# Weights loaded by thirds, k and v in two passes, one ring of PSUM double banks, more dummy matmuls and a new order of steps in an attention and maxout kernel

## The chip, the cores and the metric

One core of one Trainium2 chip. The metric is the device time of one execution in microseconds (us), median of several. A profile gives the span of one execution; the time is the span plus about 1.8 us (175.5 and 177.35 for the same execution of the kernel before). Seven of the timed runs named below count as slow, over 1.5% above the fastest of their kernel: one of e5's 20, four of e9's 20, and one of four in each of e6 and e6b. The first figure given for these kernels is the median of all runs, and that of the fast ones stands beside it; the ratios use fast runs alone. One single run that has no state is said to be so.

## The reference

```python
# q, k, v: [8 batches, 8 heads, 576, 64]; phi: [8, 8, 576, 32]; all float32
a   = softmax(phi, over the 576 positions)
k_m = a^T k;  v_m = a^T v                    # 32 memory slots for each head
attn = softmax(q k_m^T / 8) v_m
x   = attn with the heads side by side       # [4608, 512]
h   = max(x w1, x w2, x w3)                  # 768 wide
out = h w_out                                # [4608, 512]
```

## The kernel before

The kernel never forms x. It folds v_m into the weights, batch by batch, so that the softmax weights are multiplied straight with (w1 - w3), (w2 - w3) and w3 w_out. A hand-made order of steps is issued; each letter is a step, `@` gives the batch. PE does the matmuls, ACT and DVE work element by element, and POOL issues loads. A matmul writes into PSUM; to evacuate a tile is to copy it out of PSUM with ACT or DVE. The buffers of a PSUM pool are used in turn, as a ring: a new tile takes the slot of the oldest one and waits until that is evacuated. A fold is the product of v_m with one block of weight columns. What this text needs of the steps: L0, L1, L2 load phi, k with v, and q; E is exp of phi; B the k and v products; Q transposes q on DVE; S scores; M, R, X the softmax (R is ln and exp on ACT); D0 to D3 the four folds; F0 to F11 the first FFN product and its max; T0 to T4 output tiles; W and O build w3 w_out; V subtracts w3; Z is dummy matmuls that keep the clock up.

```python
acc_pool = tile_pool(name="accp", bufs=3, space=PSUM)   # double banks
one_pool = tile_pool(name="onep", bufs=2, space=PSUM)   # single banks
w_sb = const.tile([P, NP, 3, DF], BF16, name="w_sb")
# ... cut ...
load_ph(0); load_kv(0); load_q(0)       # all but phi(0) are issued by POOL, in this order
load_w(2); load w_out                   # w3, then w_out
load_w(0); load_w(1)                    # w1, w2
load_ph(1); load_kv(1); load_q(1)
# ... cut ...
EVAC = {"D": "asaa", "T": "vaava"}      # who takes folds 0..3 and output tiles 0..4 out of PSUM

def evacuate(kind, n, out_, in_):
    e = EVAC[kind][n]
    if e == "s":                                             # split: one bank each
        nc.scalar.copy(out=out_[:, 0], in_=in_[:, 0])        # ACT
        nc.vector.tensor_copy(out=out_[:, 1], in_=in_[:, 1]) # DVE
    elif e == "a": nc.scalar.copy(out=out_, in_=in_)
    else:          nc.vector.tensor_copy(out=out_, in_=in_)
# ... cut ...
for w in """
    E@0 L0@2 Z26@0 B@0 N@0 Z5@0 K@0 Q0@0 Q1@0 L2@2 L1@2 Z18@0 W1@0 W0@0 S@0 M0@0 R0@0
    W2@0 M1@0 O1@0 O0@0 V0@0 R1@0 O3@0 X0@0 X1@0 D0@0 V2@0 O2@0 F6@0 ...
""".split(): ...
for b in range(2, B - 1):
    run(b, "F6 F0 T4- F7 F4 F1 F2 F10 F3 F8 F5 F9 T2- S+ Q0++ B++ L1++++ D3+ E+++")
    run(b, "L0+++++ N++ T3- M0+ R0+ M1+ F11 X0+ T0 R1+ X1+ Q1++ L2++++ D0+ D2+ D1+")
    run(b, "T1 K++")
```

The softmax here doesn't subtract the row's maximum and nothing guards it: scores larger than these inputs give would overflow.

## Time and profile before

| | kernel before |
|---|---|
| time, median | 176.04 us (175.83 to 176.35, 3 runs) |
| profiled execution | span 175.5 us, 177.35 us with its start and end: above every timed run in this row |
| a later profile of the same kernel | span 174.0 us, 175.8 us |

The prediction shows the lines that its argument rests on. Two things that it does not show turned out to matter. The first is in the timeline of POOL, the engine that issues nearly all loads (columns: start us, length us, engine, line, what it issues, and in brackets how long POOL stood still before it and for whom):

```profile
70.66 0.76 POOL L92 DMA_DIRECT2D ph<-in_phi_dram  x1
...
80.85 0.76 POOL L92 DMA_DIRECT2D ph<-in_phi_dram  x1 [1.69 <-ACT ln L327]
...
101.52 0.74 POOL L107 DMA_DIRECT2D qq<-in_q_dram  x1 [6.08 <-DVE qT L271]
```

The last phi is issued at 80.85, and the last load of all, q, at 101.52, after it. POOL stands still for several us before a load whose buffer is not free yet; whatever is behind it in POOL's order stands still too. The second is in the list of what PE waits for, before (total us, times, longest):

```profile
PE acc L383 <- ACT wp L156: 0.9, 2, 0.7
PE acc L383 <- DVE wp L154: 0.9, 2, 0.6
```

These are the only waits for evacuated folds in the whole kernel.

### The profile page before, as it was taken

The page shows a single profiled execution, that of the slowest core. Times are in us where ns is not written, and L with a number is a line of the kernel's source. Part 1 is how long each engine was busy: PE and PEld are TensorE (multiplying, and loading weights), DVE is VectorE, ACT ScalarE, POOL GpSimd, SP SyncE. Part 2 cuts the span into 40 slices and gives each one's busy share as a digit, 9 for nine tenths or more (in the row PEclk, how much of TensorE's full clock was granted, in tenths as well). Part 3 has the DMA queues.
Part 4 walks back from the last instruction along what each step waited for, and adds up shares of the span by engine and source line. Part 5 has one row for each costly group of instructions (what it writes and reads, how often), then busy time and mean ns, then how long its engine had stood idle before and what let it go on. Part 6 is the DMA issues. An engine that isn't in the chain of part 4 may idle for free.

```text
span 175.5 us, 4464 instructions
## 1 busy us (share of the span) xinstructions
PE 162.1 (92%) x1921; PEld 89.1 (51%) x1921; DVE 103.9 (59%) x160; ACT 108.0 (62%) x162; POOL 28.3 (16%) x43
## 2 busy tenths in 40 slices
PE   7959599797999998999999999999999999999990
PEld 2334353363466544754665456547564565466430
DVE  6408216698489567767775837587748362556110
ACT  4100248945976889569949965798479648952210
POOL 7951111113303230222103010000000000000000
PEclk9999969999999999999999999999999999999999
DMA  5999999999999999999999999312013201311333
GB/s 151 169 205 209 208 211 273 212 253 232 216 320 246 238 257 246 287 236 234 321 239 277 246 250 245 100 73 108 4 63 119 86 35 63 121 60 63 119 119 121
DMA packets 21973, 31.76 MB, mean 181 GB/s; under 512 B 1216, under 2 KB 16576, under 8 KB 21952
## 3 DMA queue, kind: packets, MB, share of 16 engines
q0 software_dynamic: 16080, 21.43, 63.4%
q1 hardware_dynamic: 5728, 9.90, 16.0%
q8 instruction: 15, 0.25, 0.5%
q10 hardware_dynamic: 144, 0.13, 0.2%
q14 instruction: 6, 0.05, 0.1%
HBM read 39.32 MB, written 9.44 MB: 278 GB/s over the span
## 4 chain that ended last, share of the span: by engine, by line
PE 73%; ACT 9%; DMA 8%; DVE 4%; POOL 2%; issue 1%; DVEq 0%; POOLq 0%
PE acc L383 25%; PE po L411 24%; DMA w_sb<-in_moe_w_dram 8%; PE po L420 7%; PE wps L358 4%; PE kvp L219 3%; PE sm L314 2%; ACT wp L156 2%; PE po L175 2%; POOL kvo L99 1%; PE sc L293 1%; ACT h L393 1%; DVE hT L395 1%; PE po L429 1%; ACT r L333 1%
## 5 line engine op out<-in xcount | busy, mean ns | idle before, releaser
L383 PE MATMUL acc<-attn,wp 128*128 128x288 bf16 x384 | 52.6, 286 | 2.1 <-ACT wp L156 0.9
L411 PE MATMUL po<-wo_sb,hT 128*128 128x512 bf16 x216 | 52.6, 380 | 0.0
L395 DVE TENSOR_TENSOR hT<-acc,h 128x576 bf16<-128x576 f32 x48 | 35.1, 754 | 18.0 <-PE acc L383 12.2
L383 PEld LDWEIGHTS <-wp 128*128 128x128 bf16 x384 | 36.5, 97 | 16.2 <-issue 2.5
L393 ACT ACTIVATE h<-acc 128x576 bf16<-128x576 f32 x48 | 29.4, 652 | 12.8 <-PE acc L383 11.9
L411 PEld LDWEIGHTS <-hT 128*128 128x128 bf16 x216 | 20.0, 98 | 24.2 <-issue 4.3
L156 ACT CAST wp<-wps 128x1024 bf16<-128x1024 f32 x24 | 23.7, 1016 | 3.2 <-PE wps L358 3.2
L156 ACT COPY ot<-po 128x512 f32<-128x512 f32 x19 | 11.3, 596 | 21.2 <-PE po L420 15.7
L158 DVE COPY ot<-po 128x512 f32<-128x512 f32 x16 | 11.1, 692 | 20.2 <-PE po L420 20.2
L271 DVE STREAM_TRANSPOSE qT<-qq 128x1152 bf16<-128x1152 bf16 x16 | 21.6, 1363 | 0.6 <-DMA qq<-in_q_dram 0.6
L302 ACT ACTIVATE e<-sc 128x576 bf16<-128x576 f32 x16 | 9.6, 660 | 15.4 <-PE sc L293 15.4
L420 PE MATMUL po<-wp,attn 128*128 128x512 bf16 x64 | 19.0, 379 | 0.0
L143 PE MATMUL po<-warm 128*128 128x512 bf16 x49 | 12.7, 419 | 1.2 <-DVE warm L131 1.2
L338 DVE TENSOR_TENSOR attn<-e,r 128x576 bf16<-128x576 bf16 x16 | 12.0, 751 | 2.0 <-ACT r L333 1.9
L99 POOL DMA_DIRECT2D kvo<-in_k_dram x9 | 6.7, 747 | 31.4 <-PE kvp L219 23.4
L208 ACT ACTIVATE e<-ph 128x1152 bf16<-128x1152 f32 (+1 forms) x9 | 9.7, 1072 | 2.7 <-DMA ph<-in_phi_dram 2.7
L333 ACT ACTIVATE r<-ln 128x576 f32<-128x576 f32 x16 | 10.9, 684 | 0.5
L327 ACT ACTIVATE ln<-sm 128x576 f32<-128x576 f32 x16 | 10.3, 646 | 1.4 <-PE sm L314 1.4
L219 PE MATMUL kvp<-kvo,e 64*32 64x192 bf16 x576 | 8.4, 243 | 2.3 <-DMA kvo<-in_v_dram 2.3
L420 PEld LDWEIGHTS <-attn 128*128 128x128 bf16 x64 | 6.3, 98 | 7.0
L107 POOL DMA_DIRECT2D qq<-in_q_dram x8 | 6.0, 749 | 22.4 <-DVE qT L271 12.6
L219 PEld LDWEIGHTS <-e 64*32 64x32 bf16 x576 | 7.1, 90 | 4.1 <-issue 4.0
(43 smaller groups left out, 107.2 us busy)
## 6 DMA issues: line engine op xcount, KB each, us to landing
out_dram<-ot SPq DMA_DIRECT2D x35, 256.0 KB, 2.2
qq<-in_q_dram POOLq DMA_DIRECT2D x8, 576.0 KB, 18.1
ph<-in_phi_dram POOLq DMA_DIRECT2D x7, 576.0 KB, 17.5
kvo<-in_k_dram POOLq DMA_DIRECT2D x7, 576.0 KB, 16.2
kvo<-in_v_dram POOLq DMA_DIRECT2D x7, 576.0 KB, 19.0
w_sb<-in_moe_w_dram POOLq DMA_DIRECT2D x3, 768.0 KB, 19.7
wo_sb<-in_moe_w_out_dram POOLq DMA_DIRECT2D x1, 768.0 KB, 17.4
ph<-in_phi_dram SPq DMA_DIRECT2D x2, 288.0 KB, 3.5
```

Source lines behind the costliest of these rows:

```text
L143: nc.tensor.matmul(po[:, 0:BANK], lhsT=warm[:, 0:P], rhs=warm, start=True, stop=True)
L156: nc.scalar.copy(out=out_, in_=in_)
L158: nc.vector.tensor_copy(out=out_, in_=in_)
L219: nc.tensor.matmul(kvp[M * j : M * (j + 1), a, 0 : 3 * D], lhsT=s["e"][r, j, c, :], rhs=kv[r, :, j, c, :], start=(c == 0), stop=(c == NC - 1),
L271: nc.vector.transpose(out=s["qT"][:, j].rearrange("p j c h r -> p (j c h r)"), in_=loaded[b]["q"][:, j].rearrange("p j c d -> p (j c d)"),)
L333: nc.scalar.activation(out=r, in_=ln, func=AF.Exp, scale=-1.0)
L338: nc.vector.tensor_tensor(out=attns[b // 2][:, g, (b % 2) * S : (b % 2 + 1) * S], in0=s["e2"][:, g, 0:S], in1=s["r", g], op=ALU.mult,)
L383: nc.tensor.matmul(acc[:, h, 0:SH], lhsT=wps[b][:, g, w * DF + ft * P : w * DF + (ft + 1) * P], rhs=attn[:, g, c0 : c0 + SH], start=(g == ...
L393: nc.scalar.activation(out=h1, in_=a, func=AF.Relu)
L395: nc.vector.tensor_tensor(out=hT[:, ft, (b % 2) * S : (b % 2 + 1) * S].rearrange("p (h n) -> p h n", h=2), in0=a, in1=s["h1", ft], op=ALU.max,
L411: nc.tensor.matmul(po, lhsT=hT[:, fc, c0 : c0 + P], rhs=wo_sb[:, fc, :], start=(fc == 0), stop=False,)
L420: nc.tensor.matmul(po, lhsT=attn[:, g, c0 : c0 + P], rhs=wp3s[b][:, g, :], start=False, stop=(g == NG - 1),)
```

## The change

The intent: let weights become usable earlier, in thirds of columns that belong together; start on k while v is still under way; give output tiles and FFN tiles one common ring of PSUM; fill the early gaps of PE so that the clock stays up. With this came another division of the evacuations between ACT and DVE, and a new order of all steps. The diff is abridged.

```diff
-    tile_pool(name="accp", bufs=3, PSUM); tile_pool(name="onep", bufs=2, PSUM)
+    tile_pool(name="accp", bufs=4, PSUM)                # one ring of four double banks
-    w_sb = const.tile([P, NP, 3, DF], BF16)
+    w12 = const.tile([P, NP, NT, 2, DF // NT], BF16)    # NT = 3; w1 and w2 side by side per third
+    w3 = const.tile([P, NP, DF], BF16)
     load_ph(0)
-    load_kv(0) in halves; load_q(0); load_w(2); load w_out; load_w(0); load_w(1)
-    load_ph(1); load_kv(1); load_q(1)
+    load_q(0); load_one(k, 0); load_one(v, 0)
+    for n in 0, 1, 2: load_w(2, n); load_w(0, n); load_w(1, n)
+    load_wo(all); load_ph(1); load_q(1); load_one(k, 1); load_one(v, 1)
-    EVAC = {"D": "asaa", "T": "vaava"}
+    EVAC = {"D": "ssaa", "T": "aavaa"}
     # w_diff: one subtraction per third, w3 broadcast over w1 and w2
     # att_kv, norm, transpose: k and v separately (G, H, J) in batches 0 and 1
-    E@0 L0@2 Z26@0 B@0 N@0 Z5@0 K@0 ... Z18@0 W1@0 ...                  (49 dummies)
+    E@0 Z38@0 G0@0 Q1@0 Z9@0 G1@0 H0@0 H1@0 Q0@0 J0@0 L2@2 Z8@0 ...     (73 dummies)
+    ... M0@4 L2@7 R0@4 T1@3 X1@4 L0@7 E@6 T0@3 X0@4 K@5 L1@7            (explicit up to batch 4)
-    for b in range(2, B - 1): run(b, "F6 F0 T4- ...")
+    for b in range(4, B - 1): run(b, "F8 L2++++ F9 F6 F10 F2 F7 T4- S+ F0 F11 E+++ ...")
```

More of the change, by code (lines that the diff above doesn't have):

```diff
@@ L43 @@
     BANK = 512
+    NT = 3
+    CT = DF // NT
     const = ctx.enter_context(tc.tile_pool(name="const", bufs=1))
@@ L50 @@
     acc_pool = ctx.enter_context(
-        tc.tile_pool(name="accp", bufs=3, space=bass.MemoryType.PSUM)
-    )
-    one_pool = ctx.enter_context(
-        tc.tile_pool(name="onep", bufs=2, space=bass.MemoryType.PSUM)
+        tc.tile_pool(name="accp", bufs=4, space=bass.MemoryType.PSUM)
     )
@@ L68 @@
         kvos.append(kvo)
-    w_sb = const.tile([P, NP, 3, DF], BF16, name="w_sb")
+    w12 = const.tile([P, NP, NT, 2, DF // NT], BF16, name="w12")
+    w3 = const.tile([P, NP, DF], BF16, name="w3")
     w3T = const.tile([P, FT, NP, P], BF16, name="w3T")
@@ L92, in load_ph, with load_one, load_kv @@
             nc.gpsimd.dma_start(out=dst, in_=by_pair(phi, b))
-    def load_kv(b):
+    def load_one(src, b):
         kv = kvos[b % 2]
         loaded.setdefault(b, {})["kv"] = kv
-        for h in halves if b == 0 else [slice(0, NP)]:
-            for i, src in enumerate((k, v)):
-                nc.gpsimd.dma_start(
-                    out=kv[:, i].rearrange("p j c d -> p j (c d)")[:, h],
-                    in_=by_pair(src, b)[:, h],
-                )
+        nc.gpsimd.dma_start(
+            out=kv[:, 1 if src is k else 0].rearrange("p j c d -> p j (c d)"),
+            in_=by_pair(src, b),
+        )
+    def load_kv(b):
+        load_one(k, b)
+        load_one(v, b)
     def load_q(b):
@@ L109, in load_q, with load_w, load_wo @@
         )
-    def load_w(i):
+    def load_w(i, n):
         w = (moe_w1, moe_w2, moe_w3)[i]
+        c = slice(n * CT, (n + 1) * CT)
         nc.gpsimd.dma_start(
-            out=w_sb[:, :, i], in_=w.rearrange("(j p) f -> p j f", p=P)
+            out=w3[:, :, c] if i == 2 else w12[:, :, n, i],
+            in_=w.rearrange("(j p) f -> p j f", p=P)[:, :, c],
+        )
+    def load_wo(fs):
+        nc.gpsimd.dma_start(
+            out=wo_sb[:, fs], in_=moe_w_out.rearrange("(t p) c -> p t c", p=P)[:, fs]
         )
     load_ph(0)
-    load_kv(0)
     load_q(0)
-    load_w(2)
-    nc.gpsimd.dma_start(out=wo_sb, in_=moe_w_out.rearrange("(t p) c -> p t c", p=P))
+    load_one(k, 0)
+    load_one(v, 0)
+    load_w(2, 0)
     ident = const.tile([P, P], BF16, name="ident")
     make_identity(nc, ident)
-    load_w(0)
-    load_w(1)
+    load_w(0, 0)
+    load_w(1, 0)
+    load_w(2, 1)
+    load_w(0, 1)
+    load_w(1, 1)
+    load_w(2, 2)
+    load_w(0, 2)
+    load_w(1, 2)
+    load_wo(slice(0, FT))
     load_ph(1)
-    load_kv(1)
     load_q(1)
+    load_one(k, 1)
+    load_one(v, 1)
     warm = const.tile([P, BANK], BF16, name="warm")
@@ L139, in warm_up @@
     def warm_up(n):
-        po = one_pool.tile([P, DM], FP32, name="po", tag="one")
+        po = acc_pool.tile([P, DM], FP32, name="po", tag="acc")
         for _ in range(n):
@@ L161, in w3_t @@
     def w3_t(f2):
-        pt = one_pool.tile([P, 2, NP, P], BF16, name="pt", tag="one")
+        pt = acc_pool.tile([P, 2, NP, P], BF16, name="pt", tag="acc")
         for i in range(2):
@@ L167, in w3_t @@
                 nc.tensor.transpose(
-                    pt[:, i, j, :], w_sb[:, j, 2, f * P : (f + 1) * P], ident
+                    pt[:, i, j, :], w3[:, j, f * P : (f + 1) * P], ident
                 )
@@ L172, in w3_o @@
     def w3_o(j):
-        po = one_pool.tile([P, DM], FP32, name="po", tag="one")
+        po = acc_pool.tile([P, DM], FP32, name="po", tag="acc")
         for f in range(FT):
@@ L182, in w3_o @@
         nc.scalar.copy(out=w3o[:, j, :], in_=po)
-    w12 = w_sb[:, :, 0:2].rearrange("p j i f -> p j (i f)")
     def w_diff(n):
-        c = n * BANK
-        while c < (n + 1) * BANK:
-            e = min((n + 1) * BANK, (c // DF + 1) * DF)
-            nc.vector.tensor_tensor(
-                out=w12[:, :, c:e],
-                in0=w12[:, :, c:e],
-                in1=w_sb[:, :, 2, c % DF : c % DF + e - c],
-                op=ALU.subtract,
-            )
-            c = e
+        nc.vector.tensor_tensor(
+            out=w12[:, :, n],
+            in0=w12[:, :, n],
+            in1=w3[:, :, n * CT : (n + 1) * CT].unsqueeze(2).to_broadcast([P, NP, 2, CT]),
+            op=ALU.subtract,
+        )
     st = {}
@@ L208, in att_exp, with att_kv @@
         nc.scalar.activation(out=s["e"][:, js], in_=loaded[b]["ph"][:, js], func=AF.Exp)
-    def att_kv(b, js=range(NP)):
+    def att_kv(b, js=range(NP), slabs=slice(0, 3)):
         s = st[b]
@@ L219, in att_kv @@
                     nc.tensor.matmul(
-                        kvp[M * j : M * (j + 1), a, 0 : 3 * D],
+                        kvp[M * j : M * (j + 1), a, D * slabs.start : D * slabs.stop],
                         lhsT=s["e"][r, j, c, :],
-                        rhs=kv[r, :, j, c, :],
+                        rhs=kv[r, slabs, j, c, :],
                         start=(c == 0),
@@ L226, in att_kv, with att_k_norm @@
                     )
-    def att_kv_norm(b):
+    def att_k_norm(b):
         s = st[b]
         kvp = s["kvp"]
-        rden = work.tile([P, NG], FP32, name="rden")
+        rden = s["rden"] = work.tile([P, NG], FP32, name="rden")
         nc.vector.reciprocal(out=rden, in_=kvp[:, :, 2 * D])
-        kvn = work.tile([P, 3, P], BF16, name="kvn")
-        nc.vector.tensor_tensor(
-            out=kvn[:, 0].rearrange("p (a d) -> p a d", a=NG),
-            in0=kvp[:, :, D : 2 * D],
-            in1=rden.unsqueeze(2).to_broadcast([P, NG, D]),
-            op=ALU.mult,
-        )
+        kn = s["kn"] = work.tile([P, 2, P], BF16, name="kn")
         for g in range(NG):
-            kn = kvn[:, 1:3, HP * g : HP * (g + 1)]
             nc.vector.tensor_scalar_mul(
-                out=kn.rearrange("p h (t d) -> p h t d", t=2),
-                in0=kvp[:, g, 0:D]
+                out=kn[:, :, HP * g : HP * (g + 1)].rearrange("p h (t d) -> p h t d", t=2),
+                in0=kvp[:, g, D : 2 * D]
                 .rearrange("p (h d) -> p h d", h=2)
@@ L250, in att_kv_norm, with att_v_norm, att_kv_t @@
             )
-        s["kvn"] = kvn
-    def att_kv_t(b):
+    def att_v_norm(b):
         s = st[b]
-        ps = one_pool.tile([P, 3, P], BF16, name="kvtp", tag="one")
-        for n in range(3):
-            nc.tensor.transpose(ps[:, n], s["kvn"][:, n], ident)
-        kvt = work.tile([P, 3, P], BF16, name="kvt")
-        nc.vector.tensor_copy(out=kvt, in_=ps)
-        s["kvt"] = kvt
+        vn = s["vn"] = work.tile([P, NG, D], BF16, name="vn")
+        nc.vector.tensor_tensor(
+            out=vn,
+            in0=s["kvp"][:, :, 0:D],
+            in1=s["rden"].unsqueeze(2).to_broadcast([P, NG, D]),
+            op=ALU.mult,
+        )
+    def att_kv_t(b, k_=True, v_=True):
+        s = st[b]
+        ps = acc_pool.tile([P, 3, P], BF16, name="kvtp", tag="acc")
+        n = slice(0 if k_ else 2, 3 if v_ else 2)
+        if k_:
+            for h in range(2):
+                nc.tensor.transpose(ps[:, h], s["kn"][:, h], ident)
+        if v_:
+            nc.tensor.transpose(ps[:, 2], s["vn"].rearrange("p a d -> p (a d)"), ident)
+        if "kvt" not in s:
+            s["kvt"] = work.tile([P, 3, P], BF16, name="kvt")
+        nc.vector.tensor_copy(out=s["kvt"][:, n], in_=ps[:, n])
     def att_q(b, n):
@@ L294, in att_score @@
                             sc[a][M * j : M * (j + 1), t, 0:SH],
-                            lhsT=kvt[r, 1 + h, M * j : M * (j + 1)],
+                            lhsT=kvt[r, h, M * j : M * (j + 1)],
                             rhs=qT[r, j, :, h, :],
@@ L359, in fold @@
                     ps[M * j : M * (j + 1), a, :],
-                    lhsT=s["kvt"][r, 0, M * j : M * (j + 1)],
-                    rhs=w12[r, j, n * BANK : (n + 1) * BANK] if n < 3 else w3o[r, j, :],
+                    lhsT=s["kvt"][r, 2, M * j : M * (j + 1)],
+                    rhs=w12[r, j, n].rearrange("p i c -> p (i c)") if n < 3 else w3o[r, j, :],
                     start=True,
@@ L375, in ffn1 @@
         ft, w = n // 2, n % 2
+        k0 = (ft * P // CT * 2 + w) * CT + ft * P % CT
         if b // 2 not in hts:
@@ L384, in ffn1 @@
                     acc[:, h, 0:SH],
-                    lhsT=wps[b][:, g, w * DF + ft * P : w * DF + (ft + 1) * P],
+                    lhsT=wps[b][:, g, k0 : k0 + P],
                     rhs=attn[:, g, c0 : c0 + SH],
@@ L407, in ffn2 @@
         hT, attn = hts[b // 2], attns[b // 2]
-        po = one_pool.tile([P, DM], FP32, name="po", tag="one")
+        po = acc_pool.tile([P, DM], FP32, name="po", tag="acc")
         c0 = S - HP if t == 4 else (b % 2) * (S + HP) + t * P
@@ L458, in issue @@
             "E": lambda: [att_exp(b, h) for h in (halves if b == 0 else [slice(0, NP)])],
-            "B": lambda: [att_kv(b, range(NP)[h]) for h in (halves if b == 0 else [slice(0, NP)])],
-            "N": lambda: att_kv_norm(b),
+            "B": lambda: att_kv(b),
+            "N": lambda: (att_k_norm(b), att_v_norm(b)),
+            "G": lambda: att_kv(b, slabs=(slice(1, 3), slice(0, 1))[i]),
+            "H": lambda: (att_k_norm, att_v_norm)[i](b),
+            "J": lambda: att_kv_t(b, k_=i == 0, v_=i == 1),
             "K": lambda: att_kv_t(b),
@@ L481 @@
     for w in """
-        E@0 L0@2 Z26@0 B@0 N@0 Z5@0 K@0 Q0@0 Q1@0 L2@2 L1@2 Z18@0 W1@0 W0@0 S@0 M0@0 R0@0
-        W2@0 M1@0 O1@0 O0@0 V0@0 R1@0 O3@0 X0@0 X1@0 D0@0 V2@0 O2@0 F6@0 F2@0 F4@0 V1@0 F0@0
-        D2@0 D1@0 F7@0 F3@0 E@1 L0@3 F8@0 F1@0 F9@0 F5@0 F10@0 F11@0 B@1 L1@3 D3@0 N@1 K@1
-        D0@1 Q1@1 Q0@1 L2@3 D2@1 D1@1 T2@0 S@1 T0@0 E@2 L0@4 M0@1 R0@1 M1@1 X0@1 R1@1 X1@1
-        T3@0 T1@0 Q1@2 F0@1 F8@1 F1@1 F9@1 F6@1 F2@1 D3@1 B@2 L1@4 Q0@2 L2@4 F4@1 N@2 F7@1
-        K@2 F10@1 F3@1 S@2 F5@1 F11@1 M1@2 E@3 L0@5 M0@2 R1@2 R0@2 T0@1 D0@2 X0@2 D2@2 B@3
-        L1@5 N@3 X1@2 T1@1 D1@2 D3@2 Q0@3 Q1@3 L2@5 K@3 E@4 L0@6
+        E@0 Z38@0 G0@0 Q1@0 Z9@0 G1@0 H0@0 H1@0 Q0@0 J0@0 L2@2 Z8@0 S@0 W0@0 M1@0 V0@0 Z3@0
+        W1@0 M0@0 R1@0 J1@0 R0@0 X1@0 V1@0 X0@0 L0@2 Z12@0 D1@0 D0@0 Z3@0 F6@0 W2@0 F0@0
+        V2@0 F4@0 F7@0 F1@0 D2@0 F2@0 F3@0 Q1@1 F8@0 F10@0 O2@0 E@1 O0@0 F5@0 O1@0 L1@2 O3@0
+        F9@0 F11@0 Q0@1 D3@0 G0@1 H0@1 T3@0 J0@1 L0@3 G1@1 H1@1 J1@1 L2@3 S@1 D2@1 L1@3 T0@0
+        M1@1 Q0@2 M0@1 R1@1 T2@0 R0@1 D3@1 X1@1 X0@1 D0@1 D1@1 T1@0 F8@1 F0@1 Q1@2 F4@1 E@2
+        F9@1 F6@1 F1@1 F5@1 B@2 F2@1 L0@4 N@2 F7@1 F10@1 K@2 E@3 F3@1 L1@4 F11@1 Q1@3 S@2
+        T3@1 M0@2 R0@2 Q0@3 M1@2 T1@1 R1@2 X1@2 X0@2 T4@1 T2@1 D0@2 D2@2 B@3 N@3 D1@2 F2@2
+        F8@2 F3@2 K@3 E@4 F4@2 F9@2 F6@2 F5@2 S@3 F10@2 F7@2 L2@5 F0@2 F11@2 M0@3 F1@2 R0@3
+        M1@3 R1@3 L0@5 T0@1 D1@3 D0@3 X0@3 X1@3 D3@2 B@4 L2@4 D2@3 T1@2 L0@6 F2@3 N@4 F10@3
+        F4@3 F3@3 K@4 F0@3 F11@3 F6@3 D1@4 D3@3 Q1@4 D3@4 E@5 Q0@4 L1@5 L1@6 F8@3 T3@2 F9@3
+        T0@2 S@4 D0@4 B@5 N@5 D2@4 F5@3 L2@6 F7@3 F1@3 Q1@5 Q0@5 M1@4 T2@2 R1@4 M0@4 L2@7
+        R0@4 T1@3 X1@4 L0@7 E@6 T0@3 X0@4 K@5 L1@7
     """.split():
@@ L491 @@
         issue(int(b), n)
-    for b in range(2, B - 1):
-        run(b, "F6 F0 T4- F7 F4 F1 F2 F10 F3 F8 F5 F9 T2- S+ Q0++ B++ L1++++ D3+ E+++")
-        run(b, "L0+++++ N++ T3- M0+ R0+ M1+ F11 X0+ T0 R1+ X1+ Q1++ L2++++ D0+ D2+ D1+")
-        run(b, "T1 K++")
-    run(B - 1, "T4- F0 F2 F1 F10 F8 F11 F3 T3- F4 F6 F5 F7 F9 T2- T2 T3 T4 T0")
-    ffn2(B - 1, 1, last=True)
+    for b in range(4, B - 1):
+        run(b, "F8 L2++++ F9 F6 F10 F2 F7 T4- S+ F0 F11 E+++ T2- L1++++ M1+ R1+ F1 F4")
+        run(b, "M0+ F5 F3 R0+ T3- X0+ D0+ L0+++++ D1+ B++ D3+ N++ D2+ Q1++ X1+ T1 Q0++")
+        run(b, "K++ T0")
+    run(B - 1, "F10 F4 F5 F11 F0 F8 F6 T2- F1 F2 F9 F3 F7 T3- T2 T1 T3 T0 T4-")
+    ffn2(B - 1, 4, last=True)
 _INS = ['q', 'k', 'v', 'phi', 'moe_w1', 'moe_w2', 'moe_w3', 'moe_w_out']
```

## The prediction

> **What bounds the kernel now.** I read the page's busy lines first, then the 40 slices, then the table of windows, then the chain that ended last, and last the timeline of the first 45 us.
>
> ```profile
> PE 162.1 (92%) x1921; PEld 89.1 (51%) x1921; DVE 103.9 (59%) x160; ACT 108.0 (62%) x162; POOL 28.3 (16%) x43
> ...
> PEclk9999969999999999999999999999999999999999
> DMA  5999999999999999999999999312013201311333
> ```
>
> PE is the engine to watch, and the clock falls once, in the fifth slice. The loads keep the DMA engines full until about 110 us, so early data cannot come sooner, only in another order. Busy time overstates PE's useful work: 49 dummy matmuls (12.7 us) are in it. From windows:
>
> ```profile
> 10.00:15.00 5.00, 3.20 (x49) 1.84 (x50) 1.81 (x6) 0.00 (x0) 1.70 (x3) 1.00 1.20 208
> 20.00:25.00 5.00, 4.19 (x55) 2.50 (x53) 1.95 (x3) 2.52 (x4) 1.30 (x2) 0.66 1.18 210
> 80.00:100.00 20.00, 20.00 (x264) 11.11 (x262) 14.81 (x24) 16.29 (x25) 2.98 (x4) 1.00 1.16 265
> ```
>
> From 80 us on PE is full; early it is not. So I keep a ledger of useful PE time, with unit costs from the chain in steady state (start, us, what):
>
> ```profile
> 92.36 0.40 PE sc L293 x32
> 92.76 0.87 PE kvp L219 x72
> 93.62 0.38 PE wps L358 x8
> ...
> 95.83 0.49 PE sm L314 x4
> 96.32 0.49 PE acc L383 x4
> 96.81 1.29 PE po L411 x6
> 98.11 0.43 PE po L420 x2
> 98.54 0.77 PE wps L358 x24
> ...
> 101.14 0.17 PE kvtp L259 x3
> ```
>
> Useful work: 96 ffn1 groups x 0.49 = 47.0; 36 output tiles x 1.29 plus 32 x 0.43 and 4 x 0.55 = 62.4; per batch 0.39+0.87+0.77+0.38+0.49+0.17 = 3.07, x 8 = 24.6; 24 weight transposes x 0.057 (a third of 0.17) = 1.4; four w3o groups x 1.29 = 5.2. Sum 140.5. PE ends at 171.45, so 31.0 us are lost, and 4.05 us of evacuation and store follow. Where the loss lies, by subtracting the work done so far:
> - 28.18, first fold: done 7.2, lost 21.0.
> - 44.40, second batch's scores: done 19.0, lost 25.4.
> - 85.03, steady loop: 84.0 still to do, so done 56.5, lost 28.5.
> - end: 31.0.
>
> Two thirds of the loss are waiting for the first bytes. The timeline shows what ends it:
>
> ```profile
> 19.31 1.07 PE L167 MATMUL pt<-ident,w_sb 128*128 128x128 bf16 x16 [1.30 <-DMA w_sb<-in_moe_w_dram]
> 26.90 1.23 DVE L191 TENSOR_TENSOR w_sb<-w_sb 128x2048 bf16<-128x2048 bf16 x1 [3.10 <-DMA w_sb<-in_moe_w_dram]
> 30.61 2.43 DVE L191 TENSOR_TENSOR w_sb<-w_sb 128x2048 bf16<-128x2048 bf16 x3 [1.01 <-DMA w_sb<-in_moe_w_dram]
> 41.66 2.63 DVE L271 STREAM_TRANSPOSE qT<-qq 128x1152 bf16<-128x1152 bf16 x2
> 44.40 0.46 PE L293 MATMUL sc<-qT,kvt 32*32 32x288 bf16 x32
> ```
>
> w3 lands at 19.3, w1 at 26.9, w2 at 30.6: 768 KB each 3.7 to 3.8 us. Batch 1's scores wait for q's transpose, whose data come last.
>
> **What the Trainium skill says.** (1) "DMA: Bandwidth & Descriptors", Specifications, gives 512 B or more as the least transfer for line rate, and "Why small descriptors are slow" about three fixed cycles per packet beside 32-byte beats. A third of a row is 256 elements: 1024 B read, 512 B written, just at the limit. Three cycles on 32 beats instead of on 96 is some 6% of the thirds' 11.3 us: estimate 0.5 to 0.7 us. The trace has no such short weight rows; its 2304 B and 3072 B source rows flow equally fast per byte. (2) "TensorE: Matmul & The Clock Gate", Part 1: the clock halves after a window of about 3.4 us with little work and returns after a busy one. The trace agrees: the dummies start 0.43 us apart, later run at half that, and the granted clock is 0.66 in 20 to 25 us, after a stretch with gaps. (3) "VectorE: DVE Perf Modes", the perf-mode tier table: bf16 tensor_tensor over 2048 elements takes 1224 ns; the trace has 1.23 us. The new subtraction has the same 2048 elements with a broadcast outer dim and unit inner step, so I keep 1.23 us. (4) "PSUM — Partial Sum Buffer", Specifications: 8 banks. Before: three double plus two single; after: four double, so an output tile takes up a slot twice as large as it needs.
>
> **The change part by part.**
> *Order of loads.* q, k, v, then (w3, w1, w2) by thirds, then w_out. Landings before, against bytes asked for, give 2.83 us per q/k/v tensor, 1.26 per third, 3.77 for w_out, 1.4 for phi. So k lands at 11.8, v 14.6, first triple 18.9, second triple 23.0 (where w_out landed before), third 26.9 to 27.3, w_out 31, k of batch 1 at 38, v at 41 (where q landed before; the total is the same).
> *First fold.* Second triple 23.2, subtraction 1.23, fold at 24.5 instead of 28.18. But then only 2.8 us of useful work are done (no w3o groups): lost 21.7 instead of 21.0. The thirds alone win nothing there; they make work available sooner.
> *24.5 to 42.6.* Twelve ffn1 groups 5.9, folds 1.2, last transposes 0.5, w3o 5.2, three dummies 0.65: 13.4, plus waits for evacuated folds (0.5) and for the third subtraction (0.3) ends at about 38.5, when k of batch 1 is there. Then k part 0.9, an output tile 1.7, v at 41 and its part 0.8; the scores start at about 42.6 instead of 44.4. Useful then 18.2: lost 24.4 against 25.4. **Gain 1.0.**
> *The split.* Batches 0 and 1 have 72 more matmuls each. Batch 0's hide in the DMA wait; for batch 1, two passes of about 0.8 instead of one of 0.87: +0.7, counted above.
> *Dummies.* 73 instead of 49, 24 x 0.216 = 5.2 us more, nearly all in gaps; what they buy is the clock. At half clock, before, four w3o matmuls and eight transposes cost some 1.3 us, but w1 ended that stage anyway, so I credit nothing beyond the ledger.
> *42 to 85.* Before lost 3.1 here, waiting for max, fold and output evacuations. Walking the new order with the durations of the rows (ACT 0.65, DVE 0.75 per ffn1 tile, exp 1.2, folds 0.6 to 1.0), each tile waiting for the one four back, I find waits of 0.2 to 0.5 in a dozen places, 2.4 in all. **Gain 0.7.**
> *Steady loop.* Before, a batch takes 16.28 against 15.83 of work, and long ffn1 runs 5.60 for 11 groups instead of 5.39. In the new loop ffn1 groups are spread between output tiles, and the walk finds a free slot each time. Gain 0.2 per batch, some 0.8 to 1.0 to the end, less 0.1 as the last tile is now the one of 0.55. Fold evacuation moves 0.7 us a batch to DVE and the output evacuation moves the same back to ACT: neither is near full (59% and 62%).
> Sum: 1.0 + 0.7 + 0.8 = 2.5 us, so 176.0 becomes **173.5**.
>
> **The rivals.**
> *A. The thirds starve the queue.* If 512 B rows cost more than 6%, all landings after the weights shift; v of batch 1 then holds PE at 41. For it: PE has little else to do there, and DMA is full from 7 us. Against: the present rows show no per-row cost. Two us late would eat the gain: 175.5.
> *B. The early loss was more than DMA.* If half clock and poor packing between 28 and 85 (7.5 us lost) nearly vanish, leaving 3, the kernel ends 4 us earlier: 171 to 171.5. For it: the order looks tuned place by place. Against: batches 2 and 3 also come from a full queue; v of batch 2 lands at about 53 to 54 by my count, just when its matmuls stand (54.0, before 54.1).
> *C. One ring puts tiles behind the wrong tile.* An output tile evacuated late on ACT now holds up ffn1, which had its own banks. For it: ACT has exp, ln and reciprocal in order ahead of evacuations. Then 0.3 us a batch more: 175 to 176.
>
> **Range and chances.** My weight is mostly between main line and B on one side, A and C on the other. The bound shared by both kernels (bytes before batch 1's v, 140.5 us of work, 4 us of tail) makes more than 5 us hard to win; a loss needs A and C together. Range 170.8 to 175.8. Two per cent faster is below 172.5, which needs half of B: 0.35; within 2% 0.60; slower 0.05.
>
> **What would show each step.** In the profile after: first subtraction of the second third at 23.2 and first ffn1 matmul at 25.5 (before 30.25); w_out landing at 31; batch 1's scores at 42.6; PEclk 9 in every slice after the first; PE full from about 55, with no group of ffn1 waiting on ACT for more than 0.5 us; a steady batch of 16.0 to 16.1. Wrong: landings of the thirds more than 1.5 us apart (A); scores of batch 1 before 41 or the ledger's loss at 80 us below 25 (B); PE waits on output evacuation in the steady loop (C).

## The result, and the profile after

| | before | after |
|---|---|---|
| time, median | 176.19 us (175.83 to 176.71, 4 runs) | 181.3 us (180.91 to 183.61, 4 runs) |
| ratio after / before | | 1.0315, 95% interval 1.0224 to 1.0405 |
| profiled span | 175.5 us; 174.0 in the later profile | 179.7 us |

A ratio here and below is the record's, from the fast runs of both kernels in the same rounds, so it is not quite the ratio of the medians. The kernel became slower by 3%. The page of after, with its span, PE's busy time, the clock and the DMA share over 40 slices:

```profile
PE 163.8 (91%) x2089; PEld 91.7 (51%) x2089; DVE 102.3 (57%) x161; ACT 108.5 (60%) x170; POOL 31.4 (17%) x47
...
PEclk9999999999999999999999999999999999999998
DMA  5999999999999999999999499923011311131233
```

The clock is at 9 tenths or more in every slice but the last, in which PE's work ends, as intended. But DMA, which before was full for 24 slices in a row, has a hole in slice 23 (98.8 to 103.3 us). The list of what PE waits for in the kernel after (total us, times, longest):

```profile
PE acc L403 <- ACT ln L346: 2.4, 1, 2.4
PE po L431 <- DVE wp L172: 1.9, 5, 0.8
...
PE acc L403 <- DVE wp L172: 1.0, 3, 0.6
PE wps L377 <- DVE wp L172: 1.0, 3, 0.4
```

The kernel before has nothing like the first line, and 3.9 us now stand against DVE's half of a fold, L172, where it had 0.9 (the 0.9 for ACT is gone). The early landmarks, from the timeline of after:

```profile
23.47 1.22 DVE L204 TENSOR_TENSOR w<-w,w 128x2048 bf16<-128x2048 bf16 x1
...
43.47 0.47 PE L312 MATMUL sc<-qT,kvt 32*32 32x288 bf16 x32
```

Predicted were 23.2 and 42.6.

**Where the 2.4 us wait comes from.** One stretch of the timeline of after, engines mixed:

```profile
100.12 0.74 POOL L109 DMA_DIRECT2D qq<-in_q_dram  x1 [9.24 <-DVE qT L290]
100.85 0.76 POOL L92 DMA_DIRECT2D ph<-in_phi_dram  x1
...
112.01 1.16 ACT L220 ACTIVATE e<-ph 128x1152 bf16<-128x1152 f32 x1 [3.01 <-DMA ph<-in_phi_dram]
...
113.77 1.14 PE L403 MATMUL acc<-attn,wp 128*128 128x288 bf16 x8 [2.35 <-ACT ln L346]
```

Read it downwards. POOL stood still 9.24 us for q's buffer, which DVE frees. The phi of batch 7 is behind that q in the new order (`L2@7 ... L0@7`), so it is issued at 100.85, 20 us later than before, and lands at 112.0. ACT does its work in order: its exp of phi waits 3.01 us, and the logarithm behind it frees the PSUM slot that PE wants. PE waits 2.35 us.

**Where the waits for DVE's half come from.** A group of folds in the timeline of after:

```profile
77.83 1.08 ACT L171 CAST wp<-wps 128x512 bf16<-128x512 f32 x2
78.45 1.29 DVE L172 CAST wp<-wps 128x512 bf16<-128x512 f32 x2 [2.35 <-ACT wp L171]
...
79.19 0.41 PE L377 MATMUL wps<-w,kvt 64*32 64x512 bf16 x8 [0.28 <-DVE wp L172]
...
79.79 1.46 PE L431 MATMUL po<-wo_sb,hT 128*128 128x512 bf16 x6 [0.19 <-DVE wp L172]
```

The two halves of a split fold are in different banks and on different engines, but they do not run side by side: DVE starts 0.62 us after ACT, when ACT's first half is done, and the trace names ACT's half as what it waited for. A slot is free only after both. Before, one fold of a batch was split; now it is the first two, and the next output tile is in the same ring.

**The two profiles of before.** They differ by 1.5 us, and the prediction was built on the longer one. From the timeline of the later profile:

```profile
25.81 1.23 DVE L191 TENSOR_TENSOR w_sb<-w_sb 128x2048 bf16<-128x2048 bf16 x1 [3.74 <-DMA w_sb<-in_moe_w_dram]
...
29.50 2.43 DVE L191 TENSOR_TENSOR w_sb<-w_sb 128x2048 bf16<-128x2048 bf16 x3 [1.13 <-DMA w_sb<-in_moe_w_dram]
...
42.86 0.46 PE L293 MATMUL sc<-qT,kvt 32*32 32x288 bf16 x32
```

Here all weights land 1.1 us sooner than in the lines that the prediction shows (25.81 and 29.50 against 26.90 and 30.61), the clock does not fall, and batch 1's scores start at 42.86 instead of 44.40. So w3 landed late in the first page: POOL's issue after q's landing comes at 14.78 and 14.69 us, so that far the two agree, and the one after w3's landing at 19.81 and 18.72. The DMA engines moved 208 and 207 GB/s from 14 to 20 us, so it is not the rate; what it is, no run shows. The clock dip was at most part of the rest.

### The profile page after: what moved, and what is told of

Same layout as the page of the kernel before. It is cut to its first block, busy times and chain, and to the rows that moved or that the text cites. A ratio compares the mean times of both kernels' runs of the same rounds, so it can differ in the third digit from the quotient of the medians.

```text
span 179.7 us, 4824 instructions
## 1 busy us (share of the span) xinstructions
PE 163.8 (91%) x2089; PEld 91.7 (51%) x2089; DVE 102.3 (57%) x161; ACT 108.5 (60%) x170; POOL 31.4 (17%) x47
## 4 chain that ended last, share of the span: by engine, by line
PE 66%; DMA 12%; DVE 10%; ACT 8%; issue 2%; POOL 1%; DVEq 0%; POOLq 0%
PE po L431 23%; PE acc L403 22%; PE po L440 7%; DMA ph<-in_phi_dram 6%; DMA kvo<-in_k_dram 6%; DVE wp L172 4%; PE po L161 4%; PE po L193 3%; ACT wp L171 2%; DVE qT L290 2%; PE kvp L232 2%; PE sm L333 2%; ACT ot L174 2%; DVE hT L415 2%; PE sc L312 1%
## 5 line engine op out<-in xcount | busy, mean ns | idle before, releaser
L403 PE MATMUL acc<-attn,wp 128*128 128x288 bf16 x384 | 53.3, 286 | 3.7 <-ACT ln L346 2.4
L431 PEld LDWEIGHTS <-hT 128*128 128x128 bf16 x216 | 20.7, 98 | 24.2 <-issue 4.3
L174 ACT COPY ot<-po 128x512 f32<-128x512 f32 x27 | 15.8, 587 | 24.0 <-PE po L440 20.7
L161 PE MATMUL po<-warm 128*128 128x512 bf16 x73 | 18.1, 401 | 1.2 <-DVE warm L149 1.2
L174 ACT CAST wp<-wps 128x1024 bf16<-128x1024 f32 x16 | 15.8, 1029 | 1.4 <-PE wps L377 1.4
L172 DVE CAST wp<-wps 128x512 bf16<-128x512 f32 x16 | 10.5, 686 | 10.2 <-ACT wp L171 10.2
L161 PEld LDWEIGHTS <-warm 128*128 128x128 bf16 x73 | 7.2, 103 | 9.9 <-issue 2.1
L176 DVE COPY ot<-po 128x512 f32<-128x512 f32 x8 | 5.5, 686 | 10.6 <-PE po L440 10.6
L171 ACT CAST wp<-wps 128x512 bf16<-128x512 f32 x16 | 8.9, 596 | 3.3 <-PE wps L377 3.3
```

The source lines that it names most:

```text
L161: nc.tensor.matmul(po[:, 0:BANK], lhsT=warm[:, 0:P], rhs=warm, start=True, stop=True)
L403: nc.tensor.matmul(acc[:, h, 0:SH], lhsT=wps[b][:, g, k0 : k0 + P], rhs=attn[:, g, c0 : c0 + SH], start=(g == 0), stop=(g == NG - 1),)
L431: nc.tensor.matmul(po, lhsT=hT[:, fc, c0 : c0 + P], rhs=wo_sb[:, fc, :], start=(fc == 0), stop=False,)
```

## The experiments

Seventeen runs were made: sixteen changed kernels, and the kernel before once more (e12). The kernel before was timed beside each; its medians were 176.25 to 176.56 us. What is wanted is the cause of three losses: one around 100 to 114 us, one spread over every batch, and the early gain that did not come.

### The late phi and the split folds

**e2_phi7_early**: only the place of one load changes.

```diff
-  D2@4 F5@3 L2@6 F7@3 ... L2@7 R0@4 T1@3 X1@4 L0@7 E@6
+  D2@4 F5@3 L0@7 L2@6 F7@3 ... L2@7 R0@4 T1@3 X1@4 E@6
```

> The changed kernel with the load of phi of the last batch put ahead of the load of q of the last but one, so that it does not stand behind two loads of q which wait for VectorE. Theory L: the wait of PE for the logarithm (2.4 us at 111 us) and ACT's wait for phi (3.0 us) go, and the time falls by 2 to 3 us, to about 178.7. Theories F and R: the wait moves elsewhere and the time stays within 0.7 us of 181.3.

Measured: 179.18 us, ratio 1.0159 (1.0104 to 1.0213). From the timeline of e2:

```profile
89.47 0.76 POOL L92 DMA_DIRECT2D ph<-in_phi_dram  x1 [9.01 <-ACT e L220]
...
108.58 1.19 ACT L220 ACTIVATE e<-ph 128x1152 bf16<-128x1152 f32 x1
```

Phi is issued 11.4 us sooner, its exp waits for nothing, and the 2.4 us wait is gone from PE's list. One load behind a blocked one cost 2.1 us by the medians. This is shown, as nothing else was changed; the same edit on top of e1, in the same rounds, took off 3.2 us (e3, below).

**e1_fold_asaa**: `"D": "ssaa"` to `"asaa"` in the kernel after, the folds as before. **e3_both** is e1 with e2.

> The changed kernel with one thing undone: the first fold tile of a batch is evacuated whole by ACT again (1.0 us) instead of half by ACT (0.6) and then half by DVE (0.7). Theory F (split folds hold a slot of the ring too long, because the DVE half starts only when the ACT half has ended): the waits of PE on the DVE half (4.7 us in all) fall by half or more and the time falls by 2 to 4 us, to about 178. Theory L (late phi of the last batch): nothing but noise, within 0.5 us of 181.3. Theory R (one ring for all tiles is the fault): within 1 us of 181.3.

> Both edits. If F and L are each real and in different stretches, the gains add: 4 to 7 us, so 174.5 to 177, which is the kernel before or a little faster. If only one is real: the same as the better one of the two alone. R expects at least 179.

Measured: e1 182.63 us (1.0348, 1.028 to 1.0415), e3 179.47 us (1.0145, 1.0072 to 1.0217): no gain over the kernel after and over e2. In e3, PE still waited 2.1 us for DVE's half ahead of output tiles. One split fold is left in each batch, and it is as serial as the two were: in e1 ACT's half starts at 79.39 (0.59 us), DVE's at 80.01 (0.69 us), and the next fold on PE waits 0.28 us for it, as in the kernel after:

```profile
79.39 0.59 ACT L171 CAST wp<-wps 128x512 bf16<-128x512 f32 x1
...
79.87 2.86 ACT L174 CAST wp<-wps 128x1024 bf16<-128x1024 f32 x3
80.01 0.69 DVE L172 CAST wp<-wps 128x512 bf16<-128x512 f32 x1 [2.35 <-ACT wp L171]
```

So undoing this part of the change does not win the time back in the new order. What leaves DVE comes to ACT, whose copies of the four folds take 3.34 us from first to last here (79.39 to 82.73) and 2.91 in the kernel after (77.83 to 80.74). That this eats the gain is argued, not shown.

**e4_before_ssaa**: the other way round, the kernel before with `"D": "ssaa"`.

> The kernel before with one part of the change alone: its first fold tile is split as well, ACT half and then DVE half. Theory F: slower by 1 to 3 us, 177 to 179, with waits of PE on the DVE half that the kernel before did not have. If the split costs only in the one shared ring (theory R), the kernel before, with its two separate rings, stays at 176.2 within 0.5.

Measured: 179.6 us, 1.0172 (1.0125 to 1.0219). So the second split fold alone costs the kernel before, in its own order, 3 us. In its profile the FFN tiles waited six times for DVE's half (1.7 us) and batch 1's scores 1.7 us for the transpose of q, which is behind that half on DVE.

**e5_vaaa**: e2, with the first fold whole on DVE and the other three whole on ACT: `"D": "ssaa"` to `"vaaa"`. Nothing is split.

> The changed kernel with phi of the last batch loaded early and with no fold tile split: the first goes whole to VectorE, the second whole to ScalarE, so that the two run side by side. The first trial (only the first fold unsplit, by ScalarE) did not help because an output copy 0.59, fold one 0.91, fold two's half 0.5 and VectorE's half 0.7 then stand in one row, 2.7 us behind the last output tile, against 2.4 when both are split. Theory F2 (what costs is the length of that row, since the next output tile takes the slot of the second fold): with 1.2 on VectorE beside 0.6 + 0.9 on ScalarE the row is 1.5 to 1.8 us, PE arrives after 1.7 to 1.9, the waits of PE for the folds fall from 3.9 us to under 1, and the time falls by 2.5 to 3.5 us against the run with early phi alone (179.2), to about 176. If the folds are not what costs: 179 within 0.7.

Measured: 177.17 us (20 runs; 177.16 for the 19 fast ones), 1.0049 (1.0027 to 1.0072), 2.0 us below e2. The same group of folds in the timeline of e5:

```profile
78.14 2.85 ACT L174 CAST wp<-wps 128x1024 bf16<-128x1024 f32 x3
78.25 1.23 DVE L176 CAST wp<-wps 128x1024 bf16<-128x1024 f32 x1 [1.83 <-PE wps L377]
...
79.21 0.41 PE L377 MATMUL wps<-w,kvt 64*32 64x512 bf16 x8
```

DVE begins 0.11 us after ACT, on another fold, and the next fold on PE follows without a wait. The Trainium skill agrees: "PSUM — Partial Sum Buffer", Specifications, says that ScalarE and VectorE can access PSUM in parallel at full bandwidth as long as they are not on the same bank. So the serial halves need not be put down to PSUM; the trace shows a wait of DVE's half for ACT's, and why the program has it, no run shows. ACT's row of fold copies is as long here as in the kernel after (2.85 us, 78.14 to 80.99, against 2.91), so the 2.0 us are not won by a shorter row on ACT but with DVE taking out its fold beside ACT. No run has split folds whose halves do run side by side, which would be the direct test.

### The ring and the dummies

**e6_two_rings**: e2 with the PSUM pools of before (three double banks, two single ones for dummies, transposes and output tiles). **e6b_two_rings_vaaa**: the same with `"vaaa"`.

> The changed kernel with early phi and its split folds, but with the PSUM of the kernel before: three double slots for the attention, fold and ffn1 tiles, two single ones for output tiles, weight transposes and dummies. Theory R (the one ring makes an output tile wait for the evacuation of a fold): the wait of an output tile's matmuls for VectorE's half (1.9 us) goes, the time falls by 1 to 2.5 us against 179.2. Theory F2 alone, without the ring: no gain, and folds now wait for tiles only three back, so it may be slower by up to 2 us.

> Both: two rings and whole folds on two engines, with early phi. If the one ring costs only through the folds, it is the same as whole folds in one ring within 0.7 us (176). If three double slots are too few for this order, it is slower than that by 1 us or more. If the ring costs on top, it is faster by 1 us or more, under 175.

Measured: 192.15 us (1.0878, 1.0798 to 1.0957) and 189.38 us (1.0723, 1.0665 to 1.0782); their three fast runs each have medians of 191.15 and 189.34. The theory that the one ring itself costs time fell: the new order needs it, by 12 us (against e2 and e5). That is no verdict on one ring in general, as the order was made for it.

**e7_no_gap_dummies**: e5 without `Z9 Z8 Z3 Z12 Z3`, the 35 dummies in the gaps; the first 38 stay.

> Early phi and whole folds in one ring, without the 35 dummy matmuls in the gaps (the first 38 stay). If they only fill gaps and the clock does not matter there: the time is unchanged within 0.7 us. If they keep the clock: granted clock under 0.95 somewhere between 10 and 35 us, and up to 2 us slower. If they stand in the way of work that is ready (the three ahead of the first ffn1 group wait 0.65 us): faster by up to 0.7 us.

Measured: 178.79 us (4 runs), 1.0142 (1.0075 to 1.0209), 1.6 us more than e5. The clock line of its page:

```profile
PEclk9997555899999999999999999999999999999997
```

Five slices in a row are below 9, where e5 and the kernel after have none before the last slice. (This profile is the slowest of the four runs, and its loads came 1.0 us later than those of e5: the second subtraction at 24.61 against 23.62. The 1.6 us are from the medians.) The prediction's second point from the Trainium skill is borne out: the dummies buy what they were meant to buy.

### The early part

**e8_w3_whole**: e5 with w3 in one load, then w1 and w2 in thirds, then w_out; the rest as in e5.

> With early phi and whole folds (177.2), but w3 loaded whole ahead of the thirds of w1 and then those of w2, so the second triple is complete only with the second third of w2. By the bytes ahead of it that is 3 thirds later, 3.8 us at the rate of the profile (1.26 us a third). If the order by thirds really pays: first fold 3 to 4 us later, and the time 1.5 to 3 us longer (some of the delay is filled by w3's transposes). If what follows is bound by PE's work and by later loads: within 0.7 us of 177.2.

Measured: 180.89 us, 1.0246 (1.016 to 1.0332), 3.7 us more than e5. PE waited 3.1 us for a subtraction, and the clock fell to 6 tenths in one slice. Within this order of steps, taking the thirds in turn is worth those 3.7 us.

**e9_k_first**: e5 with k and v ahead of q, and batch 0's steps and dummies dealt out anew. **e10_batch1_unsplit**: e5 with batch 1's k and v in one pass, and an output tile in the gap.

> With early phi and whole folds (177.2), but k and v of the first batch loaded ahead of q, as in the kernel before, and the dummies dealt out anew. In all seven profiles of the changed kernel and its variants all of PE's work up to 50 us stands at a fixed distance from the first k matmul, 12.0 to 13.6 us. If the landing of k sets that pace: first k matmul at about 9.5, and the time 1 to 3 us shorter. If the landing of the second triple of weights sets it (23.2, the same bytes ahead of it in either order): the first fold at about 24.5 instead of 25.0, and at most 0.7 us gained.

> With early phi and whole folds (177.2), but batch 1's k and v in one pass again, and an output tile in the gap before the scores. The prediction put the split at +0.7 us. If it costs that and hides nothing: 0.5 to 1 us faster. If the split lets the scores start before v is there: slower by up to 1 us.

Measured: 177.05 us (1.002, 0.9997 to 1.0043) and 177.44 us (1.0053, 1.0033 to 1.0073), 20 runs each (176.89 for the 16 fast ones of e9): no clear change from e5. In e9 k's products began at 10.44 instead of 12.44 us, and the first fold at 25.32 instead of 25.00: the second triple of thirds sets it, not k. The split of k and v is worth nothing here and costs nothing that can be seen.

**e12_before_again**: the kernel before, unchanged, for a second profile (one run, no state).

> The kernel before once more, for a second profile. Its timed runs lie at 175.4 to 177.7 and its first profiled run was 1.3 us over the median: I expect the same intervals between stages as in the first profile from 45 us on, and only the first 45 us to differ, by up to 1.5 us.

Measured: 175.8 us, span 174.0; its lines are shown above.

**e13_before_third_rows**: the kernel before, with the three weights still in its own order, but each in three loads of a third of the columns.

```diff
-  dma_start(out=w_sb[:, :, i], in_=w)
+  for n in range(3):
+      c = slice(n * DF // 3, (n + 1) * DF // 3)
+      dma_start(out=w_sb[:, :, i, c], in_=w[:, :, c])
```

> The kernel before, its weight loads alone cut in thirds of columns and kept in the old order w3, wo, w1, w2. If the narrower rows are what makes the early loads later, each of the three weights lands some 6% later than in the second profile of before (3.7 to 3.8 us each there), so w2 lands 0.5 to 0.7 us later than 29.5 us, and the time is 0.4 to 0.7 us above before (ratio 1.002 to 1.004). If the rows cost nothing and the early loss is of order alone, the last weight lands at 29.5 and the ratio is 1.000.

Measured: 177.62 us (6 runs), 1.0076 (1.0045 to 1.0107): slower by 1.4 us, more than expected. The last subtractions, in its timeline, start 1.6 us later than the 29.50 of e12:

```profile
31.08 2.43 DVE L193 TENSOR_TENSOR w_sb<-w_sb 128x2048 bf16<-128x2048 bf16 x3 [2.63 <-DMA ph<-in_phi_dram]
```

From w_out's landing to this start it took 8.06 us (23.02 to 31.08) against 7.45 in e12 (22.05 to 29.50): 0.3 us more for each of the two weights. (The bracket names phi's load; releasers are inferred, and by the program this subtraction needs only weights.) The kernel after agrees: POOL's issues, each released by the landing of a third, come 1.34 us apart (16.63 to 23.31 us, five steps), where a third of a whole weight takes 1.25 us (3.7 to 3.8 us for all). That is about the 6% of the prediction, and it recurs nine times. A fixed cost for each load instead of each row would leave a dip between loads; from 23.0 to 28.6 us of e13 40 equal steps of the DMA rate show none, all between 183 and 212 GB/s with a mean of 196, against a mean of 210 with whole rows (e12, 22.0 to 27.75). w_out itself came 1.0 us later in this profile, which may be the late landing of the first page of before; the profile does not tell. So the narrow rows cost 0.6 us of this at least, and the whole cut 1.4.

### The early part of before with the later order of after

**e14_hybrid**: loads and steps of before up to output tile T3 of batch 0, then the later order of after, one ring, `"vaaa"`, phi early. **e15_hybrid_guard**: three dummies after the first scores.

> Early stage, loads and weight products of the kernel before up to the transposes of batch 0, then the changed kernel's later order, with one ring of four double banks, folds on DVE and ACT side by side (vaaa), outputs aavaa, and phi of the last batch loaded early. Theory that the losses add: 23.8 us lost up to the scores of batch 1 as in the second profile of before, and 1.0 us less than before from there on, so about 175.2 us, ratio 0.993 to 0.996. Rival, that the one ring breaks the early order of before, which was made for two rings: 177 us or more, ratio above 1.002.

> As e14_hybrid, with three dummy groups after the first scores, where the page of before showed the granted clock fall to 6 tenths for a slice. If that dip comes in a part of the executions and costs 1.5 us each time, the median falls by up to 0.7 us against e14_hybrid and the spread of its runs narrows to below 1 us. If the dip has another cause, the same time as e14_hybrid, or 0.3 us more for the added work.

Measured: 178.86 us (1.016, 1.0132 to 1.0189) and 178.37 us (1.0135, 1.0112 to 1.0157). Both lie in the range of the rival, but its reason was not the right one. The timeline of e14:

```profile
29.77 1.22 DVE L155 CAST wp<-wps 128x1024 bf16<-128x1024 f32 x1
31.01 2.43 DVE L188 TENSOR_TENSOR w_sb<-w_sb 128x2048 bf16<-128x2048 bf16 x3
...
46.55 0.47 PE L290 MATMUL sc<-qT,kvt 32*32 32x288 bf16 x32 [1.63 <-DVE qT L268]
```

A whole fold on DVE now stands ahead of w2's subtraction, and another one, at 42.73, ahead of the transpose of q, for which batch 1's scores wait 1.63 us.

**e16_hybrid_fold** and **e17_hybrid_fold_guard**: the same two, with the folds of batches 0 and 1 evacuated as `"asaa"`.

> As e14_hybrid, but the folds of batches 0 and 1 are evacuated as in the kernel before (first on ACT, second split, the rest on ACT) and only later batches use DVE for the first fold. In e14_hybrid a 1.22 us fold on DVE stood ahead of the subtraction of w2 (31.01 instead of 29.77) and another 1.23 us one ahead of q's transposes (43.87), for which batch 1's scores waited 1.63 us. If these two are why the hybrid lost, the scores of batch 1 come 2.0 to 2.9 us earlier and the time is 176.0 to 176.6, ratio 0.998 to 1.002. If the one ring is the reason, at most 1 us is gained: 177.5 or more.

> As e16_hybrid_fold, with the three dummies after the first scores. The same time within 0.5 us (the guard gained 0.5 at most between the two hybrids before): 175.7 to 176.6. Below 175.5 would beat the kernel before; above 177.5 speaks for the one ring as the cause of the early loss.

Measured: 176.91 us (1.0034, 1.0017 to 1.0051) and 176.97 us (1.0041, 1.0028 to 1.0054), 22 runs each. In e16 the subtraction starts at 29.15 and the scores at 42.24 us, 4.3 us sooner than in e14; of this 1.9 us are e14's later w3 (19.72 against 17.84), and the other 2.4 go with the two folds. The ring was not to blame. Yet only 2.0 us arrive at the end, by the medians. Part of the lead is lost by batch 3's scores: they start at 72.19, which is also where e5 has them, though e5's batch 1 scores come at 43.55; DVE waits 4.15 us before them for batch 3's q to land:

```profile
62.75 2.64 DVE L268 STREAM_TRANSPOSE qT<-qq 128x1152 bf16<-128x1152 bf16 x2 [4.15 <-DMA qq<-in_q_dram]
```

The guard dummies are worth nothing. None of the sixteen changed kernels beats the one before.

## Why the prediction was wrong

The prediction had PE end 2.5 us before the page's 171.45, at 168.95; it ended at 175.63. Three kernels with the same later order, split at the start of a batch's scores, divide the difference (all from the traces; the end is the last matmul's):

| us | predicted | after | e2 | e5 |
|---|---|---|---|---|
| batch 1 scores start | 42.6 | 43.47 | 43.18 | 43.55 |
| batch 5 scores | | 106.67 | 106.38 | 105.21 |
| batch 6 scores | | 126.04 | 122.97 | 121.36 |
| batch 7 scores | | 144.57 | 141.50 | 139.45 |
| PE ends | 168.95 | 175.63 | 172.56 | 170.47 |
| scores of batch 1 to the end | 126.35 | 132.16 | 129.38 | 126.92 |

So: 0.87 us from the late start, 132.16 - 129.38 = 2.78 from the late phi, 129.38 - 126.92 = 2.46 from the split folds, and 126.92 - 126.35 = 0.57 unexplained; together 6.68. All of the 2.78 lies between the scores of batches 5 and 6 (19.37 us in after, 16.59 in e2). These are single profiles; by the medians of the timed runs the late phi cost 2.1 and the folds 2.0. The remaining 1.1 us of the 7.8 between 173.5 and 181.3 comes from the page of before: its execution was 1.3 us above the median that I took as the start, so its losses were too large for a typical run (the profile of after is 0.2 us above its own median). And the kernel before takes 127.05 and 127.07 us from batch 1's scores to the end in its two profiles: even with both faults mended, e5's 126.92 is only level with it.

**Two readings**: the clock of the page of before falls in the sixth of the 40 slices (21.9 to 26.3 us), not in the fifth. And the line of q's transposes at 41.66 has no wait in it: DVE comes to them straight from a copy at 41.38, and q, issued at 14.78 to 15.52 with 25.7 us to landing, was there at 40.5 to 41.2. So the scores of batch 1 waited for transposes that stood behind other work on DVE, and that q's data held them is not shown.

**Loads and first subtraction**: right. 23.47 against 23.2, a third every 1.34 us, the 6% about as estimated.

**24.5 to 42.6, gain 1.0**: wrong in what it is compared with. The scores came 0.9 us earlier than in the page of before, but 0.6 later than in its second profile, with 0.8 us less work done (18.2 against 19.0). PE's list of after has no wait for a load in this stretch, so v's landing at 41 did not hold the scores as the prediction had it. e13 shows that cutting the rows alone costs before 1.4 us; the gain was to pay for that and did not. e9 and e10 show that neither k's place nor the split of batch 1 decides it.

**The split, and the dummies**: partly right. Batch 1's two passes took 0.83 and 0.75 us, about as assumed, but the +0.7 does not show in the time: e10, without the split, is no faster than e5. The dummies hold the clock, and e7 puts 1.6 us on the 35 in the gaps of e5, where I had credited nothing beyond the ledger. As the kernel after has them and still lost, this did not move the balance.

**42 to 85 and the steady loop, gains 0.7 and 0.8**: this is the step that failed. The walk of the order "finds a free slot each time" and gives 126.35 us from batch 1's scores to the end; 132.16 were measured. It had two terms wrong. First, "folds 0.6 to 1.0": that holds for a split fold only if its halves run side by side, and they run one after the other and take 1.31 us (79.39 to 80.70 in e1). PE waited 3.9 us for DVE's halves in the kernel after. Second, every load was taken to be there: the landings that the prediction counts end with v of batch 2, so it never met phi of batch 7 behind a q that stood 9.24 us. No group of ffn1 was to wait for ACT for more than 0.5 us; one waited 2.35. The Trainium skill has the rule in "TensorE: Matmul & The Clock Gate", in the specification table's row on queue depth: GpSimd's queue is strict first in, first out; the trace agrees, and I had not looked it up for POOL. Without both faults the walk was not bad: e5's batch takes 16.15 us (105.21 to 121.36) against the predicted 16.0 to 16.1, before 16.28; e2, with the halves, 16.59.

**The rivals.** A did not come: the thirds came 1.34 us apart, not more than 1.5, and PE did not wait for v of batch 1. B fell: nothing of the early loss vanished. C came nearest in its place, output tiles waiting in the common ring, but with another cause: e6 shows that the ring is needed, and e5 that the tiles wait for a split fold. C's size, 0.3 us a batch, was close to the 0.44 of e2 against e5. The chance of 0.05 for a slower kernel was too small: it was reasoned that A and C would have to come together, and the fault lay in a queue that neither looked at.

**What stays open**: the 0.57 us; why one split fold fewer wins nothing in e1; what makes the weights land 1.1 us late in some executions; and how the 1.4 us of e13 divide between rows and chance.

## What to carry to other kernels

When a new order moves loads, walk the issuing engine's own queue to its last load, and ask of each load that waits for a buffer what is stuck behind it. Splitting an evacuation over two engines frees the slot sooner only if the trace shows the halves side by side; giving whole tiles to either engine was 2 us faster here (e5), while undoing one of the two splits on ACT won nothing (e1); and each copy put on DVE also delays what is behind it there. Take two profiles of the kernel before, and start the sum from the one whose time is nearer the median.

## What the Trainium skill lacked or had wrong

- "DMA: Bandwidth & Descriptors", Specifications and "Why small descriptors are slow": 512 B as the least transfer for line rate is not quite met by rows of 1024 B read and 512 B written: a third every 1.34 us against 1.25 us from whole rows. The fixed cost of three cycles per packet, worked out in the prediction as 6%, fits. The cut cost the kernel before 1.4 us in all (e13), of which the rows explain 0.6.
- "TensorE: Matmul & The Clock Gate" states that GpSimd's queue is strict first in, first out, but no page draws the consequence for loads issued from it: a q held 9.24 us for its buffer made a phi behind it late, 2.8 us in the profiles and 2.1 by the medians.
- "PSUM — Partial Sum Buffer", Specifications: parallel access by ScalarE and VectorE is borne out by e5 (both at work from 78.25 us). No page warns that a copy split over the two, in two different banks, may be serialised by the program's own waits (0.62 us between the starts; e2 with split folds against e5 without: 2.5 us in the profiles, 2.0 by the medians).
- No page gives a figure for how far the landing of the same loads differs between executions of one kernel: w1 landed at 25.81 or 26.90 us, and the span was 174.0 or 175.5 us.
